# A different order at four places in the start of an attention and FFN kernel on one Trainium2 core

## Chip, core and metric

The kernel runs on one core of a Trainium2 chip. The metric is the device time of one execution, in microseconds (us). Ten runs of the kernel before have a median of 182.95 us (182.34 to 186.69).

## What is computed

Windowed attention with four sink keys, then a feed-forward layer of three matrices of which the elementwise maximum is taken. Cut to what matters:

```python
# batch 4, heads 8, seq 768, head_dim 64; n_sink 4, window 128
scores = (1 / np.sqrt(D)) * np.matmul(q, k.transpose(0, 1, 3, 2))
keep = is_sink | in_window            # key < 4, or 0 <= query - key < 128
scores = np.where(keep, scores, -1e9)
a = np.exp(scores - np.max(scores, axis=-1, keepdims=True))
a = a / (np.sum(a, axis=-1, keepdims=True) + 1e-09)
x = np.matmul(a, v)                   # (B, H, S, D), laid out as 3072 x 512
h = np.maximum(np.maximum(x @ w1, x @ w2), x @ w3)   # 512 x 768 each
out = h @ w_out                       # 3072 x 512
```

Inputs and output are float32; the kernel multiplies in bf16.

## The kernel before

The 3072 tokens are cut into 12 chunks of 256, three to a batch. A chunk goes through these steps, each of which is a letter in strings that write out the order of the work by hand (`step`, L453; `run`, L494). A string such as `"Fb8 Vc Ac0"` with `b=1, c=2` means FFN piece 8 of chunk 1, then the sinks' values of chunk 2, then head pair 0 of chunk 2.

- K, Q (L227, and L240 for the chunks 1 and 2): K and Q are turned on TensorE (PE) into PSUM, and copied to SBUF. K is copied by DVE (VectorE), Q mostly by ACT (ScalarE, L236 and L256).
- B, S (L283, L291): scores of a pair of heads on PE (L306) and their exp on ACT (L312). For the chunks 0 and 1 the mask is added by PE ahead of the scores (L288); later it is multiplied in on DVE (M, L319).
- Z (L321): scores of the sink keys and their exp, for chunks that are not the first of a batch.
- V (L337): eight small matmuls (L345) start four output tiles, one for each head pair, with the sinks' values.
- A (L349): attention times values of a head pair (L358), then on DVE the reciprocal of the sum (L363) and the product that gives x (L366).
- T (L371): x is turned, on PE for the chunks 0 to 4 (L381), by DMA later.
- F (L389): one of nine pieces of the hidden layer, eight matmuls each (L396). The piece's number divided by 3 gives the 256 columns, the rest gives the matrix. The first matrix's result is copied by ACT (L400), the others are joined by a maximum on DVE (L402).
- Y, W (L410): twelve matmuls with w_out (L417) for the two halves of a chunk, copied by ACT (L423) and stored over SP's DMA queue (L407).

The order in the text is the order of issue on every engine: each engine takes its instructions in that order and waits on semaphores for the others. All PSUM tiles come from one pool of eight banks; a tile has to wait until the last reader of its bank's former tile is done.

Transfers go over two queues. SP loads K, Q (L70) and v (L93) of chunk 0, then the rows of v that belong to the sinks (L110). Pool (GpSimd) issues those that cast to bf16 or come early: K and Q of chunks 1 and 2 as `runs` (L84), v of chunks 1 and 2 (L93), the three hidden matrices `w` (L162) and w_out (L170). At the start Pool also makes the identity, the masks (L135 to L146) and, in `sink_v_init` (L178), a selection matrix `sel` (L179, L183) with a column of ones (L180). PE uses `sel` in `sink_v` (L186) to spread the sinks' values over partitions.

`warm(n)` (L124) issues n matmuls of the identity with itself, whose result is not used.

Of the kernel before, what the change touches and what calls it, by code (L numbers as in the profile page):

```python
# [16 lines left out]
def kernel(  # L17
# [33 lines left out]
    with tc.manual_schedule():  # L51
# [26 lines left out]
        def load_runs(ci):  # L78

            b, c = divmod(ci, CPB)  # L80
            t0 = c * 256
            runs[ci] = raw.tile([128, 2, 16 * D], BF16, tag="runs", bufs=2, name="runs")
            for j, src in ((0, k), (1, q)):
                nc.gpsimd.dma_start(  # L84
                    out=runs[ci][:, j],
                    in_=src[b, :, t0:t0 + 256].rearrange("h (r x) d -> h r (x d)", x=16))
            raws[ci] = [None]
# [10 lines left out]
        def load(ci, gate=None):  # L98
            load_qk(ci, gate)
            load_v(ci)  # L100
# [23 lines left out]
        def warm(n):  # L124

            wp = psum.tile([128, 128], F32, tag="f", name="warm")
            for _ in range(n):
                nc.tensor.matmul(wp, lhsT=ident, rhs=ident, start=True, stop=True)  # L128
# [29 lines left out]
        def load_w(wi, lo=0, hi=d_ff):  # L158

            w = (moe_w1, moe_w2, moe_w3)[wi]  # L160
            wt = const.tile([128, DS, hi - lo], BF16, name=f"w{wi}_{lo}")
            nc.gpsimd.dma_start(out=wt, in_=w[:, lo:hi].rearrange("(a p) f -> p a f", p=128))  # L162
            for fb in range(lo // 128, hi // 128):
                w_sb[wi, fb] = wt[:, :, fb * 128 - lo:fb * 128 - lo + 128]
# [3 lines left out]
        def load_wo():  # L168
            for a in range(2):
                nc.gpsimd.dma_start(  # L170
                    out=wo[:, 3 * a:3 * a + 3],
                    in_=moe_w_out[384 * a:384 * a + 384].rearrange("(a p) f -> p a f", p=128))
# [5 lines left out]
        def sink_v_init():  # L178
            nc.gpsimd.memset(sel, 0.0)  # L179
            nc.gpsimd.memset(v_sink[:, :, D:D + 1], 1.0)  # L180
            idv = ident[0:R, 0:R].rearrange("r (s p h) -> r p s h", p=NP, h=2)
            for h in range(2):
                nc.gpsimd.tensor_copy(sel[:, h, :, 0:2 * n_sink].rearrange(  # L183
                    "r p (s h) -> r p s h", h=2)[:, :, :, h], idv[:, :, :, h])

        def sink_v():  # L186
            for h in range(2):
                pv = psum.tile([128, B, D + 1], F32, tag="f", name="vs_ps")
                nc.tensor.matmul(pv, lhsT=sel[:, h].rearrange("r p x -> r (p x)"), rhs=v_sink,
                                 start=True, stop=True)  # L190
                nc.vector.tensor_copy(vs[:, :, h], pv)
# [3 lines left out]
        def cast_qk(ci, j, g, eng):  # L195
            if ci not in bfs:
                bfs[ci] = raw.tile([128, 2, 2, 2, 256], BF16, tag="qk_bf", name="qk_bf")
            src = raws[ci][0][:, j, g].rearrange("p (h i d) -> p h i d", h=4, d=D)
            if ci <= CPB:
                dst = bfs[ci][:, j, g]  # L200
            else:
                dst = bfs[ci][:, j].rearrange("p i a x -> p i (a x)")[:, :, 256 * g:256 * g + 256]
            (eng.tensor_copy if eng else nc.scalar.copy)(  # L203
                dst.rearrange("p i (h d) -> p h i d", d=D), src)
# [10 lines left out]
        def cast(ci):  # L215
            for j, g in ((0, 0), (1, 0), (0, 1), (1, 1)):
                cast_qk(ci, j, g, nc.gpsimd)
            for n in range(2):
                cast_v(ci, n, nc.gpsimd)
# [233 lines left out]
        def step(op):  # L453

            name, ci, arg = op[0], int(op[1:3]), op[3:]
            if ci >= NCH:
                return
            if name in "KQ":
                (prep_runs if ci in runs else prep)(ci, int(name == "Q"), int(arg))
            elif name == "D":  # L460
                turn(ci)
            elif name == "L":
                load(ci)
            elif name == "E":
                place_k(ci, kTs.pop(ci), slice(0, NP))
            elif name == "S":
                score(ci, [int(x) for x in arg])
            elif name == "B":
                score_banks(ci, [int(x) for x in arg])
            elif name == "M":  # L470
                mask(ci, [int(x) for x in arg])
            elif name == "Z":
                if ci % CPB:
                    sink_score(ci)
            elif name == "X":
                if ci % CPB == 0:
                    sink_k(ci // CPB)
            elif name == "V":
                if ci % CPB:
                    sink_av(ci)  # L480
            elif name == "A":
                av(ci, int(arg))
            elif name == "T":
                xpose(ci, int(arg))
            elif name == "F":
                ffn_h(ci, int(arg))
            elif name == "Y":
                ffn_y(ci, [int(arg)], [range(FB)])
            elif name == "W" and ci == NCH - 1:
                ffn_y_end(ci)  # L490
            elif name == "W":
                ffn_y(ci, [0, 1], [range(4), range(4, FB)])

        def run(text, **at):  # L494
            for tok in text.split():
                c = at[tok[1]]
                step(f"{tok[0]}{c:02d}{tok[2:]}")

        sink_v_init()
        load_runs(1)
        load_v(1, nc.gpsimd)
        load_w(0, 0, 256)
        load_w(0, 256, d_ff)
        warm(36)
        cast_qk(0, 0, 0, nc.vector)
        cast_qk(0, 1, 0, nc.vector)
# [18 lines left out]
        load_runs(2)  # L527
        load_v(2, nc.gpsimd)
        load_wo()
        warm(3)  # L530
        run("Aa0 Aa1 Aa2 Aa3 Kb0 Qb0 Ta0 Ta1 Bb01 Sb01 Zb", a=0, b=1)
        sink_v()
        run("Bb23 Sb23 Fa0 Vb Ab0 Ab1 Fa3 Ab2 Ab3 Fa6 Fa1 Tb0 Tb1 Fa4", a=0, b=1)
        cast_v(2, 0, nc.gpsimd)
# [3 lines left out]
            a=0, b=1, c=2)  # L538
# [1 line left out]
        nc.gpsimd.memset(ve[1][:, :, :, D:D + 1], 1.0)  # L540
        cast(3)
        load(4)
        run("Fb5 Sc23 Mc23 Vc Ac0 Fb8 Ac1 Ya0 Ya1", a=0, b=1, c=2)
        cast(4)
        run("Ac2 Ac3 Yb0 Tc0 Tc1 Kd0 Qd0 Yb1 Kd1 Qd1", b=1, c=2, d=3)
        run("Zd Sd0123 Md0123 De Lf", d=3, e=4, f=5)

        for i in range(2, NCH):
# [51 lines left out]
```

## Time and profile before

| What | Value |
|---|---|
| Median of 10 runs | 182.95 us |
| The profiled execution | 183.39 us |
| Its span, first to last instruction | 181.3 us |
| Granted PE clock | 0.995 |
| Chain that ended last, by engine | PE 76%, DMA 11%, SP's queue 3%, ACT 3%, DVE 2% |
| Pool's `sink_v_init` (L179 to L183) | 4.80 to 5.72 us |
| Pool's first five DMA issues | 5.72 to 9.85 us |
| `runs` of Q of chunk 1 land | 13.01 us |
| v of chunk 0 lands | 9.10 us |
| w1, columns 256 to 767, lands | 24.13 us |

The profile is of one execution. A row of a timeline gives the start and the length in us, the engine, the line, the operation, what it writes and reads, how many instructions were merged, and in brackets the idle time of the engine just before and what ended it. PEld is the load of PE's weights, which lies beside its matmuls. The chain of waits is followed back from the last instruction: at each step to what released it, or to the instruction before it on its engine. A row of windows has for each engine the busy time and the number of instructions in that stretch, then the granted PE clock, the mean busy share of the 16 DMA engines (over 1 where packets overlap) and what they moved in GB/s. All times count from the start of the span.

### The profile page before, as it was taken

The page shows a single profiled execution, that of the slowest core. Times are in us where ns is not written, and L with a number is a line of the kernel's source. Part 1 is how long each engine was busy: PE and PEld are TensorE (multiplying, and loading weights), DVE is VectorE, ACT ScalarE, POOL GpSimd, SP SyncE. Part 2 cuts the span into 40 slices and gives each one's busy share as a digit, 9 for nine tenths or more (in the row PEclk, how much of TensorE's full clock was granted, in tenths as well). Part 3 has the DMA queues.
Part 4 walks back from the last instruction along what each step waited for, and adds up shares of the span by engine and source line. Part 5 has one row for each costly group of instructions (what it writes and reads, how often), then busy time and mean ns, then how long its engine had stood idle before and what let it go on. Part 6 is the DMA issues. An engine that isn't in the chain of part 4 may idle for free.

```text
span 181.3 us, 4873 instructions
## 1 busy us (share of the span) xinstructions
PE 170.9 (94%) x1974; PEld 131.9 (73%) x1985; DVE 115.7 (64%) x245; ACT 90.1 (50%) x191; POOL 70.0 (39%) x121
## 2 busy tenths in 40 slices
PE   6969989999999999999999999999999999999991
PEld 6645878775697688588597588687796796796880
DVE  1686435687289289597576676686595786663451
ACT  2447742562971872951933913914736626522220
POOL 7995700657802395454024525326236200000001
PEclk9999999999999999999999999999999999999997
DMA  5999999999599999991789999798999933222404
GB/s 143 237 184 202 208 207 250 199 291 286 151 177 255 189 238 315 250 286 41 141 246 255 148 257 250 154 302 207 130 287 240 125 95 61 45 74 58 116 0 116
DMA packets 64645, 33.63 MB, mean 185 GB/s; under 512 B 26640, under 2 KB 60944, under 8 KB 64624
## 3 DMA queue, kind: packets, MB, share of 16 engines
q1 hardware_dynamic: 59520, 27.70, 65.6%
q0 software_dynamic: 4864, 5.38, 16.5%
q10 hardware_dynamic: 240, 0.26, 0.6%
q8 instruction: 15, 0.25, 0.5%
q14 instruction: 6, 0.05, 0.1%
HBM read 25.20 MB, written 6.29 MB: 174 GB/s over the span
## 4 chain that ended last, share of the span: by engine, by line
PE 76%; DMA 11%; SPq 3%; ACT 3%; issue 2%; DVE 2%; POOL 1%; POOLq 0%; ACTq 0%
PE h_ps L396 49%; PE y_ps L417 15%; DMA w<-in_moe_w_dram 7%; PE o_ps L358 5%; PE st L306 3%; DMA xT<-x_sb 2%; DMA vs_raw<-in_v_dram 2%; ACT e_sb L312 2%; PE y_ps L436 1%; DVE h_sb L402 1%; SPq L110 1%; SPq L70 1%; PE o_ps L345 1%; PE xt_ps L381 1%; PE pt L251 1%
## 5 line engine op out<-in xcount | busy, mean ns | idle before, releaser
L396 PE MATMUL h_ps<-xT,w 128*128 128x256 bf16 x864 | 103.4, 273 | 1.4 <-DMA w<-in_moe_w_dram 0.8
L396 PEld LDWEIGHTS <-w 128*128 128x128 bf16 x864 | 81.1, 98 | 13.6 <-issue 1.6
L402 DVE TENSOR_TENSOR h_sb<-h_sb,h_ps 128x512 bf16<-128x512 bf16 x72 | 49.1, 684 | 27.6 <-PE h_ps L396 23.2
L312 ACT ACTIVATE e_sb<-st 128x512 bf16<-128x512 f32 (+1 forms) x96 | 45.2, 598 | 6.5 <-PE st L306 6.5
L400 ACT CAST h_sb<-h_ps 128x512 bf16<-128x512 f32 x36 | 21.9, 613 | 47.2 <-PE h_ps L396 47.2
L203 POOL CAST qk_bf<-qk_raw 128x512 bf16<-128x512 f32 x36 | 22.4, 630 | 47.0 <-DMA qk_raw<-in_k_dram 27.6
L319 DVE TENSOR_TENSOR e_sb<-e_sb,msk 128x1024 bf16<-128x1024 bf16 (+1 forms) x40 | 28.0, 703 | 18.5 <-ACT e_sb L312 18.2
L212 POOL CAST ve<-v_raw 64x512 bf16<-64x512 f32 x44 | 30.6, 695 | 23.8 <-DMA v_raw<-in_v_dram 19.7
L417 PE MATMUL y_ps<-wo,h_sb 128*128 128x512 bf16 x121 | 30.1, 379 | 0.9
L417 PEld LDWEIGHTS <-h_sb 128*128 128x128 bf16 x132 | 12.4, 97 | 14.1 <-issue 1.1
L366 DVE TENSOR_TENSOR x_sb<-o_ps,rc 128x256 bf16<-128x256 f32 x48 | 20.4, 424 | 1.7
L358 PE MATMUL o_ps<-ve,e_sb 128*128 128x65 bf16 x352 | 17.8, 193 | 1.3 <-DVE ve L212 1.3
L358 PEld LDWEIGHTS <-e_sb 128*128 128x128 bf16 x352 | 15.7, 97 | 3.4 <-issue 0.8
L423 ACT COPY y_sb<-y_ps 128x512 f32<-128x512 f32 x22 | 12.6, 635 | 9.8 <-PE y_ps L417 9.7
L407 POOL DMA_DIRECT2D out_dram<-y_sb x1 | 0.6, 571 | 35.4 <-ACT y_sb L447 35.4
L306 PE MATMUL st<-qT,kk 64*128 64x128 bf16 (+1 forms) x256 | 13.5, 237 | 0.5 <-ACT qT L236 0.3
L306 PEld LDWEIGHTS <-kk 64*128 64x128 bf16 x256 | 8.8, 94 | 4.7 <-issue 2.7
L363 DVE RECIPROCAL rc<-o_ps 128x4 f32<-128x4 f32 x48 | 8.4, 176 | 4.8 <-PE o_ps L358 4.7
L128 PE MATMUL warm<-ident 128*128 128x128 bf16 x43 | 4.7, 298 | 1.4 <-POOL ident masks.py:199 1.4
L330 ACT ACTIVATE e_sink<-sk 128x256 bf16<-128x256 f32 x8 | 3.2, 395 | 5.6 <-PE sk L325 5.6
L256 ACT CAST qT<-pt 128x512 bf16<-128x512 f32 x4 | 2.1, 588 | 7.6 <-PE pt L251 7.6
L383 ACT COPY xT<-xt_ps 128x512 bf16<-128x512 bf16 x8 | 4.3, 594 | 2.1 <-PE xt_ps L381 2.1
(58 smaller groups left out, 76.2 us busy)
## 6 DMA issues: line engine op xcount, KB each, us to landing
out_dram<-y_sb SPq DMA_DIRECT2D x22, 256.0 KB, 4.1
qk_raw<-in_k_dram SPq DMA_DIRECT2D x20, 256.0 KB, 4.0
qk_raw<-in_q_dram SPq DMA_DIRECT2D x20, 256.0 KB, 4.6
v_raw<-in_v_dram SPq DMA_DIRECT2D x10, 512.0 KB, 5.9
v_raw<-in_v_dram POOLq DMA_DIRECT2D x2, 512.0 KB, 10.4
w<-in_moe_w_dram POOLq DMA_DIRECT2D x2, 512.0 KB, 11.4
w<-in_moe_w_dram POOLq DMA_DIRECT2D x1, 768.0 KB, 14.9
wo<-in_moe_w_out_dram POOLq DMA_DIRECT2D x2, 384.0 KB, 14.2
```

The source lines that it names most:

```text
L203: (eng.tensor_copy if eng else nc.scalar.copy)(dst.rearrange("p i (h d) -> p h i d", d=D), src)
L212: (eng.tensor_copy if eng else nc.scalar.copy)(dst[64 * i:64 * i + 64], src[64 * n:64 * n + 64, :, i])
L306: nc.tensor.matmul(st[h][:, sl], lhsT=kx[r, p, k0:k0 + 128], rhs=qx[r], start=ci >= 2, stop=True, skip_group_check=ci < 2)
L312: nc.scalar.activation(e[:, h, lo:], st[:, lo:], AF.Exp, scale=scale)
L319: nc.vector.tensor_tensor(out=e, in0=e, in1=m, op=ALU.mult)
L358: nc.tensor.matmul(o[:, t, h], lhsT=es[ci, p][:, h, sl], rhs=ve[b % 2][:, n, 2 * p + h], start=(c == 0 and x == 0), stop=(x == len(blocks) ...
L366: nc.vector.tensor_mul(xs[ci][:, :, 2 * p:2 * p + 2], o[:, :, :, 0:D], rc.unsqueeze(3).to_broadcast([128, 2, 2, D]))
L396: nc.tensor.matmul(hp[:, f], lhsT=w_sb[wi, 2 * fp + f][:, ds], rhs=xTs[ci][:, :, ds], start=(ds == 0), stop=(ds == DS - 1))
L400: nc.scalar.copy(dst, hp)
L402: nc.vector.tensor_max(dst, dst, hp)
L417: nc.tensor.matmul(yps[ci, t], lhsT=hs[ci][:, fb, t * 128:(t + 1) * 128], rhs=wo[:, fb], start=(fb == 0), stop=(fb == FB - 1))
L423: nc.scalar.copy(y[:, t], yps.pop((ci, t)))
```

## The change

Four things are put in another order, and thirteen warm-up matmuls are added.

```diff
-        sink_v_init()
         load_runs(1)
         load_v(1, nc.gpsimd)
         load_w(0, 0, 256)
         load_w(0, 256, d_ff)
+        sink_v_init()
         warm(36)
...
         load_wo()
-        warm(3)
-        run("Aa0 Aa1 Aa2 Aa3 Kb0 Qb0 Ta0 Ta1 Bb01 Sb01 Zb", a=0, b=1)
+        warm(8)
+        run("Aa0 Aa1 Aa2 Aa3", a=0)
+        warm(8)
+        run("Kb0 Qb0 Ta0 Ta1 Bb01 Sb01 Zb", a=0, b=1)
         sink_v()
...
-        run("Fb5 Sc23 Mc23 Vc Ac0 Fb8 Ac1 Ya0 Ya1", a=0, b=1, c=2)
+        run("Fb5 Sc23 Mc23 Fb8 Vc Ac0 Ac1 Ya0 Ya1", a=0, b=1, c=2)
         cast(4)
-        run("Ac2 Ac3 Yb0 Tc0 Tc1 Kd0 Qd0 Yb1 Kd1 Qd1", b=1, c=2, d=3)
+        run("Ac2 Ac3 Yb0 Tc0 Tc1 Kd0 Qd0 Kd1 Qd1 Yb1", b=1, c=2, d=3)
```

First, Pool makes the selection matrix after it has issued the transfers of chunk 1 and of the first hidden matrix. Second, eight warm-up matmuls instead of three stand ahead of the values of chunk 0 (`Aa`), and eight more between them and the turning of K of chunk 1 (`Kb0`). Third, the last FFN piece of chunk 1 (`Fb8`) stands ahead of the sink values and the first head pair of chunk 2 (`Vc Ac0`). Fourth, the second half of K and Q of chunk 3 (`Kd1 Qd1`) is turned ahead of the second half of y of chunk 1 (`Yb1`).

## Prediction

> **What bounds the kernel now.** I read the page first, then the chain of waits in order of time, then what TensorE (PE) waits for, then the timeline of the three places that the change touches, and last the busy time and DMA traffic in short windows there.
>
> ```profile
> PE 170.9 (94%) x1974; PEld 131.9 (73%) x1985; DVE 115.7 (64%) x245; ACT 90.1 (50%) x191; POOL 70.0 (39%) x121
> ...
> DMA  5999999999599999991789999798999933222404
> ```
>
> PE is busy for 94% of the span, so time comes only out of its few waits. DMA is near full for the first 33 us.
>
> ```profile
> PE o_ps L358 <- DVE ve L212: 1.3, 2, 0.7
> PE h_ps L396 <- DMA w<-in_moe_w_dram: 0.8, 1, 0.8
> PE pt L251 <- DMA runs<-in_q_dram: 0.5, 1, 0.5
> PE st L306 <- ACT qT L236: 0.3, 1, 0.3
> PE o_ps L345 <- DVE h_sb L402: 0.2, 1, 0.2
> ```
>
> Each row: who waited, for what, us in total, times, longest. These are all of PE's waits from 9 to 62 us. Later it waits once more, 0.4 us for a transposed x.
>
> ```profile
> 11.92 12.21 DMA w<-in_moe_w_dram
> 24.13 0.05 issue
> 24.18 7.16 PE h_ps L396 x64
> ```
>
> In the chain the second part of w1 lands at 24.13 and PE goes on at 24.18, after 0.76 us of idling. PE had run out of other work at 23.26, or 23.2 without a wait of 0.1 for w0 at 19.69; so everything before 24.18 has nearly 1 us of slack. From 24.18 the chain is PE nearly without a break. A shift there reaches the end unless a transfer catches it.
>
> **First part: the selection matrix goes behind Pool's first DMA issues.** L179 to L184 take Pool from 4.80 to 5.72, so the five issues (runs of K and Q of chunk 1, v of chunk 1, both parts of w0) move up by 0.92 us. Behind them the last of these issues ends at 8.93 instead of 9.85; the init then runs to 9.85, and the cast of v_sink (9.85 before), the copies of ks and the issues of w1 and w2 follow as before. Were this stretch 0.3 to 0.5 us longer (the four ks copies of 8 columns take 0.98 us beside DVE's casts of v), it would cost nothing: Pool's queue is still moving w0 until 19.65, so the w1 issued at 11.19 waits in line anyhow. The same holds if SP's sink loads, for which that cast waits (landed 9.32), come 0.5 later. `sel` is first read at 15.87.
>
> What do 0.92 us buy? The packets of the trace put the first data of Pool's queue at 7.58 (1.86 us after the issue) and the last of SP's first loads at 8.49. In between the engines fall idle:
>
> ```profile
> 6.50:7.50 1.00, 1.00 (x12) 0.67 (x12) 0.71 (x3) 0.24 (x1) 1.00 (x2) 1.00 1.17 332
> 7.50:8.00 0.50, 0.50 (x12) 0.30 (x9) 0.50 (x2) 0.30 (x1) 0.50 (x1) 1.00 1.29 228
> 8.00:8.50 0.50, 0.50 (x7) 0.33 (x5) 0.34 (x2) 0.50 (x3) 0.50 (x2) 1.00 0.71 138
> 8.50:9.00 0.50, 0.50 (x9) 0.21 (x8) 0.16 (x1) 0.50 (x3) 0.50 (x2) 1.00 0.60 99
> ```
>
> The last two columns are DMA share and GB/s: 332 while SP's queue runs alone, 228 with both, 99 while Pool's first transfer is alone on about half of the engines. Filling the hole at 8 to 9.2 should bring w1 forward by most of the 0.92 us. The bounds are 0.3 (Pool's early packets get in only between SP's) and 0.92; I take 0.7, so w1 would land at 23.4.
>
> Two rules of the Trainium skill speak against it. "SBUF — State Buffer", section "Who interferes with whom", says that a DVE instruction in a two-port mode keeps GpSimd from writing descriptors. The first issue would now start at 4.80, under DVE's cast of 4.69 to 5.12; by the rule 0.32 of the 0.92 us is lost. The rows: the runs' issues took 756 and 712 ns beside DVE casts here, and 642 and 616 ns at 18 us with DVE idle. By the rows the loss is 0.1 per issue, and the early issues pay that already. I follow the rows.
>
> The second matters more. "DMA: Bandwidth & Descriptors", "Queues, rings and completion order", says that each DMA engine goes round-robin between queues that have work. Pool's packets, starting at 6.66, would then take from SP's v of chunk 0, for which DVE waits:
>
> ```profile
> 9.12 1.96 DVE L212 CAST ve<-v_raw 64x512 bf16<-64x512 f32 x4 [0.46 <-DMA v_raw<-in_v_dram]
> 9.21 0.17 PEld L128 LDWEIGHTS <-ident 128*128 128x128 bf16 x3 [0.16 <-issue]
> ```
>
> v lands at 9.10; DVE casts until 11.08, makes x of chunk 0 until 13.71, turns K of chunk 1 until 14.91, and PE scores chunk 1 at 15.10. That chain has no slack, so a late v delays PE by as much. By the rule's equal shares, the 1.05 us of SP data left at 6.66 (702 packets of 512 B, at 85 KB per 0.25 us) takes twice as long: about 1.0 later. By the trace, the 172 packets left at 7.59 (0.3 us of work alone) took 0.9, which is a third of the speed on the slowest engines; if much of that was the small sink loads queued behind, it was two thirds. That gives 0.2 to 1.15 us; no row lies nearer to one end, so I take 0.65. PE would reach the w1 matmuls at 23.2 + 0.65 = 23.85, after w1's landing at 23.4. Part one is thus 23.85 - 24.18 = **-0.33**, and by the bounds from -0.75 (v 0.2 late, w1 decides) to +0.2 (v 1.15 late).
>
> **Second part: more warm-up matmuls.** Warm ones are 57 ns apart (0.17 us for three). Five more before AV of chunk 0 are 0.28 us, in the 0.58 us in which PE waits for `ve` at 9.55 to 10.13. The eight new ones ahead of K of chunk 1 are 0.45 us, at 11.87. Before, K took 11.87 to 12.49 and Q waited for its runs until 13.06. Now K would run 12.32 to 12.94 and Q at once, if its runs land by 12.9 (13.01 less about 0.7). The next step, turning x, waits for DVE until 13.71 anyhow. All this moves with v alike, so I cost it at nothing. Without that cover it would be 0.45. Below nothing it could go only by keeping a clock that would else drop; the granted clock is 1.00 from 5.3 to 175 us, so no such gain is due.
>
> **Third part: the last FFN piece of chunk 1 (Fb8) ahead of AV of chunk 2.**
>
> ```profile
> 38.63 0.23 PE L345 MATMUL o_ps<-vs,e_sink 32*128 32x130 bf16 x2
> 39.10 0.39 PE L345 MATMUL o_ps<-vs,e_sink 32*128 32x130 bf16 x6 [0.24 <-DVE h_sb L402]
> ```
>
> The eight sink matmuls need four PSUM banks. Two are free, the third comes with DVE's max at 39.04, the fourth with an exp at 39.17. From 38.63 to the next matmul at 39.42 pass 0.79 us; the same eight took 0.22 at 18.72. So 0.57 us are lost, of which the wait view shows 0.24. Fb8, now at 39.70, is 0.88 us on PE (8 by 110 ns). Put first, it finds one of the two free banks and runs 38.63 to 39.51. The sink matmuls follow, with the exp's bank long free and the last one coming from Fb5's max at 39.64, 0.1 late. I take **-0.5**, bounds 0 and -0.57. On DVE the max of Fb8 moves ahead of the normalisation of the first two head pairs; that row ends at 43.10 before and after, since the masks hold DVE until 41.40. x of chunk 2 would be ready by about 44.45, when PE comes for it at 44.6.
>
> **Fourth part: K and Q of chunk 3 turned ahead of y of chunk 1.** Eight transposes (0.45 us) swap with six y matmuls (1.3 us).
>
> ```profile
> 47.56 0.59 ACT L423 COPY y_sb<-y_ps 128x512 f32<-128x512 f32 x1
> ...
> 48.05 0.59 ACT L236 COPY qT<-pt 128x512 bf16<-128x512 bf16 x1
> ...
> 48.69 0.51 PE L306 MATMUL st<-qT,kk 64*128 64x256 bf16 x8 [0.28 <-ACT qT L236]
> ```
>
> The second half of the scores waits 0.28 us for the copy of Q, which stood behind ACT's copy of y. Turned early, Q is copied under the y matmuls and the wait goes. But the same ACT time now lies in the copy of y, ahead of the eight exps. The next FFN matmul (49.13) needs the bank that the first exp frees at 49.03. Without the wait PE would come at about 48.8, and the exps start at most 0.05 earlier. So the wait changes its name. I take **-0.05**, bounds 0 and -0.28.
>
> **The sum.** -0.33 + 0 - 0.5 - 0.05 = -0.88 us. The profiled execution took 183.39 (span 181.3, so 2.1 around it); it would be 182.5. The median of the runs is 182.95, and becomes 182.1.
>
> **Rivals.**
> *The start gives nothing* (0.2): v of chunk 0 is late by 0.9 us or more and eats the slack, or a later transfer (xT lands 4.3 us after its issue at 98 us) swallows part. Then some 0.5 is left: 182.45.
> *Fb8 gets the bank of Fb5* (0.1), free at 39.64. It starts at 39.70 as before, with sink and AV work behind it (0.11 + 0.26 + 0.24): y starts at 41.18 instead of 40.81, 0.37 late, which cancels the start: 183.0. Against it: two banks were seen free at 38.63, and the first taker gets one.
> *SP's v is starved* (0.1), the slower end. Where the queues share, Pool's first transfers are served first (16 packets of 173 ns on each of its engines, 2.8 us). v would be some 2.4 us late; 0.9 is slack, 1.5 comes on top, less the 0.55 of the other parts: 183.9. It decides from 1.45 us on. Against it: at 7.6 to 8.5 SP's packets advanced at a third of their speed at worst.
> *As summed* (0.6): 182.1.
>
> About 0.3% (0.55 us) is what a measurement here can tell from no change, so the border is 182.4. Faster: nearly all of the sum's 0.6 and half of the first rival, 0.67; slower: the starved v and a little of the others, 0.12; the rest same. The range reaches from the lower bounds of all parts (-0.75 - 0.57 - 0.28 = -1.6) to a v that is 1.9 late (1.0 beyond the slack, less 0.55: +0.45): 181.4 to 183.4.
>
> **What would show it.** Pool's first issue at 4.80, SP's v landing at 9.3 to 10.3 and the cast at L212 with it; the h_ps matmuls after the turn of x starting near 23.85, with the DMA wait of 0.8 gone or short; eight sink matmuls in about 0.25 us with no DVE wait; no wait on qT at the second half of the scores, but about 0.2 us before the next h_ps. I am wrong if v lands beyond 10.6, if PE shows a new wait of over 0.3 us between 15 and 50 us, or if PE's lead at 50 us is gone by the end.

## The result, and the profile after

The kernel after has a median of 181.19 us (180.65 to 182.56, 15 runs), beside 183.03 (182.21 to 186.69, 50 runs) for the kernel before. The ratio is 0.9907, 95% interval [0.9887, 0.9927]. So it is faster, as forecast, but by 1.7 us (from the ratio) to 1.8 us (from the medians) where 0.88 was forecast, and the time lies below the range of 181.4 to 183.4. The profiled execution took 181.71 us, span 180.0, against 183.39 and 181.3. So the time outside the span fell as well, from 2.1 to 1.7 us. The ratios of this document leave out executions more than 1.5% above the fastest of their kernel; the medians keep them.

The same two rows of the page, and the row of an instruction queue that the prediction did not look at:

```profile
PE 171.7 (95%) x1986; PEld 132.9 (74%) x1998; DVE 116.5 (65%) x245; ACT 90.1 (50%) x191; POOL 69.5 (39%) x121
...
DMA  4999999999599999993789999999999934122404
...
q8 instruction: 15, 0.25, 0.6%
```

PE has a little more to do (the 13 warm-ups) in a span that is 1.3 us shorter. All that PE still waits for between 9 and 70 us, in the view of waits (who, for what, us in total, times, longest):

```profile
PE o_ps L358 <- DVE ve L212: 1.4, 2, 0.8
PE o_ps L345 <- DVE h_sb L402: 0.2, 1, 0.2
```

The waits for w1, for Q's runs and for qT are gone. The sinks' wait for DVE is still there.

**The start.** Pool's timeline:

```profile
4.71 0.76 POOL L84 DMA_DIRECT2D runs<-in_k_dram  x1
5.46 0.61 POOL L84 DMA_DIRECT2D runs<-in_q_dram  x1
6.05 0.95 POOL L93 DMA_DIRECT2D v_raw<-in_v_dram  x1
6.99 1.52 POOL L162 DMA_DIRECT2D w<-in_moe_w_dram  x2
8.55 0.30 POOL L179 MEMSET sel<- 32x256 bf16 x1
...
12.34 0.40 POOL L520 CAST v_sink<-vs_raw 32x256 bf16<-32x256 f32 x1 [3.08 <-DMA vs_raw<-in_v_dram]
```

The issues start where they were expected. The cast of v_sink waits 3.08 us for the sink rows behind SP's v and runs at 12.34 instead of 9.85, so w1 is issued 2.1 us later (13.30, before 11.19). That is more than the 0.3 to 0.5 us for which the prediction had argued that it costs nothing. It costs nothing all the same: w1 lands at 22.51, 1.62 us earlier than before. The chain of waits (start, length) shows what takes the place of w1:

```profile
21.74 1.75 PE h_ps L396 x16
23.48 0.24 PE xt_ps L381 x4
23.72 0.02 issue
23.74 1.08 ACT xT L383 x2
24.82 0.04 issue
24.87 1.14 PE h_ps L396 x9
```

PE reaches the w1 matmuls at 23.77 (forecast 23.85, before 24.18). After the first eight it needs the turned x of chunk 1, which ACT has copied only at 24.82. The next one starts 0.34 us after the eighth, where two usually lie 0.11 apart. That wait was hidden under the wait for w1. By starts of single FFN pieces, the lead is 0.41 us at 23.8 and 0.20 from 26 us on.

**The third and the fourth part.** PE's timeline at the sinks:

```profile
38.44 1.05 PE L396 MATMUL h_ps<-xT,w 128*128 128x256 bf16 x8
39.41 0.23 PE L345 MATMUL o_ps<-vs,e_sink 32*128 32x130 bf16 x3
39.80 0.27 PE L345 MATMUL o_ps<-vs,e_sink 32*128 32x130 bf16 x5 [0.15 <-DVE h_sb L402]
40.00 0.66 PE L358 MATMUL o_ps<-ve,e_sb 128*128 128x65 bf16 x16
```

The eight sink matmuls still take 0.59 us, from 39.41 to 40.00. The y matmuls begin at 40.50, before at 40.81. With the lead of 0.20 taken off, the third part gave 0.11 here on PE's path instead of 0.5. ACT's timeline at the fourth place:

```profile
46.50 1.11 ACT L236 COPY qT<-pt 128x512 bf16<-128x512 bf16 x2
47.70 0.59 ACT L423 COPY y_sb<-y_ps 128x512 f32<-128x512 f32 x1
48.18 1.65 ACT L312 ACTIVATE e_sb<-st 128x384 bf16<-128x384 f32 x4
```

Both copies of Q now stand ahead of the copy of y; the next FFN matmul starts at 48.73 (before 49.13), and the lead is 0.41 us from 53 to 100 us.

**Late in the kernel.** The rest of the gain lies where nothing was changed. The chain at 100 us, of before:

```profile
98.24 4.31 DMA xT<-x_sb
102.55 0.14 issue
102.69 1.36 PE h_ps L396 x11
```

and of after:

```profile
99.56 2.32 PE y_ps L417 x10
101.88 2.19 PE h_ps L396 x20
```

Before, PE stands still for 0.55 us until the x that DMA has turned lands. (I count such a wait as the time from the last y matmul to the next FFN matmul, less the 0.216 that lies between two y matmuls.) Two more such waits, 0.24 us at 154.7 and 0.11 at 166.5, have no row in the view of waits. After, the three are 0.01, 0.00 and 0.02. So of the span's 1.32 us, 0.41 are from the four places and about 0.9 from these waits.

**Outside the span.** The two profiled executions differ by 1.68 us, their spans by 1.32. The rest, some 0.35 us, lies outside the first and last instruction. The experiments say which part it belongs to.

### The profile page after: what moved, and what is told of

Its sections match the earlier page's. It is cut to its first block, busy times and chain, and to the rows that moved or that the text cites. A ratio compares the mean times of both kernels' runs of the same rounds, so it can differ in the third digit from the quotient of the medians.

```text
span 180.0 us, 4899 instructions
## 1 busy us (share of the span) xinstructions
PE 171.7 (95%) x1986; PEld 132.9 (74%) x1998; DVE 116.5 (65%) x245; ACT 90.1 (50%) x191; POOL 69.5 (39%) x121
## 4 chain that ended last, share of the span: by engine, by line
PE 84%; DMA 4%; DVE 4%; ACT 3%; issue 2%; SPq 1%; ACTq 0%
PE h_ps L396 50%; PE y_ps L417 16%; PE o_ps L358 6%; DMA v_raw<-in_v_dram 4%; PE st L306 3%; ACT e_sb L312 2%; DVE h_sb L402 2%; PE y_ps L436 2%; PE pt L251 1%; PE xt_ps L381 1%; SPq L70 1%; PE o_ps L345 1%; PE st L288 1%; DVE ve L212 1%; PE sk L325 1%
## 5 line engine op out<-in xcount | busy, mean ns | idle before, releaser
L319 DVE TENSOR_TENSOR e_sb<-e_sb,msk 128x1024 bf16<-128x1024 bf16 (+1 forms) x40 | 29.5, 744 | 18.7 <-ACT e_sb L312 18.0
L128 PE MATMUL warm<-ident 128*128 128x128 bf16 x56 | 5.9, 287 | 1.4 <-POOL ident masks.py:199 1.4
L128 PEld LDWEIGHTS <-ident 128*128 128x128 bf16 x56 | 5.1, 135 | 1.6 <-POOL ident masks.py:199 1.4
```

What stands on the lines that cost most here:

```text
L319: nc.vector.tensor_tensor(out=e, in0=e, in1=m, op=ALU.mult)
```

## The experiments

Two theories for the part of the gain that I had not forecast. In the expectations they are CLOCK and FETCH.

*Clock.* The ten runs before reach from 182.34 to 186.69. In some executions PE's clock is halved for a while, because PE idles too much ahead of the values of chunk 0. More warm-ups prevent it. (This theory came up after the first four runs.)

*Fetch.* PE reads its instructions through a queue of its own: 15 packets of 16 KB (the row of q8). The times of these packets are in the trace's list of packets, in no view. One lies at 98.3 and one at 152.6 us in before, while x is being turned by DMA. Thirteen more matmuls (26 instructions) bring each fetch forward, to 95.4 and 149.4 in after.

The rivals: the parts give all of it on PE's path, and the late waits are chance (PLACES); or any lead at 24 us brings the later loads forward and so ends the late waits (EARLY).

All runs came in three sets, with 75, 29 and 25 executions of before beside them (medians 183.17, 182.96, 183.20). A halving of 3.4 us takes about 1% off the mean granted clock of an execution (1.7 us of 181), and the half clock at the very end, after PE's last matmul, up to 0.5%; "dropped" counts those below 0.9925.

| Kernel | Median us | Ratio to before [95%] | Dropped | Median of the rest |
|---|---|---|---|---|
| p1_sel: part one alone | 183.01 | 0.9994 [0.9966, 1.0022] | 7 of 22 | 182.70 |
| p2_warm: part two alone | 182.56 | 0.9957 [0.9934, 0.9980] | 0 of 22 | 182.56 |
| p3_fb8: part three alone | 182.40 | 0.9955 [0.9935, 0.9976] | 3 of 22 | 182.21 |
| p4_turn: part four alone | 182.93 | 0.9972 [0.9952, 0.9993] | 4 of 22 | 182.90 |
| before, beside these four | 183.17 | | 19 of 75 | 182.91 |
| a_nosel: after without part one | 181.82 | 0.9935 [0.9915, 0.9956] | 0 of 6 | 181.82 |
| a_nowarm: after without part two | 182.34 | 0.9885 [0.9843, 0.9927] | 4 of 7 | 180.54 |
| c_late13: before, 13 warm-ups at 23 us | 182.71 | 0.9985 [0.9965, 1.0005] | 0 of 22 | 182.72 |
| a_fa7: after, one FFN piece earlier | 181.66 | 0.9924 [0.9894, 0.9953] | 0 of 7 | 181.66 |
| before, beside these four | 182.96 | | 2 of 29 | 182.96 |
| r_after: after, once more | 181.54 | 0.9891 [0.9866, 0.9916] | 0 of 6 | 181.53 |
| p12: parts one and two | 182.31 | 0.9941 [0.9908, 0.9975] | 1 of 10 | 182.04 |
| a_late13: after, part two's 13 at 23 us | 182.14 | 0.9943 [0.9915, 0.9971] | 7 of 16 | 181.30 |
| a_gap16: after, all 16 ahead of AV | 181.71 | 0.9904 [0.9880, 0.9928] | 0 of 6 | 181.72 |
| before, beside these four | 183.20 | | 4 of 25 | 183.05 |

**Each part alone.** p1_sel moves only `sink_v_init`:

```diff
-        sink_v_init()
         load_runs(1)
...
         load_w(0, 256, d_ff)
+        sink_v_init()
```

> The kernel before with the first part alone (selection matrix behind Pool's first issues). Three theories. PLACES: each part gains where it stands, and the 0.9 us by which turned x came late at 102, 155 and 167 us in the profile of before is chance of that one execution. Then the time is 0.2 to 0.3 us under before (ratio 0.9985). FETCH: the late turns of x come from a 16 KB fetch of PE's instructions that falls on them; only the 26 added PE instructions (13 warm-up matmuls with their weight loads) move the fetches. Then this kernel too gains 0.2 to 0.3, and its trace still has a fetch near 98 us and a wait for x of about 0.5 there. EARLY: whatever brings PE forward by 0.3 us at 24 us brings the loads forward and ends the late waits: then 0.9 to 1.2 us faster (ratio 0.994).

The median gains 0.16 us and the ratio's interval covers 1; the executions without a drop gain 0.2, and a third drop. In its trace PE is 1.07 us ahead at 26 us, and at 102 us it waits 0.65 us for the turned x. So a lead alone doesn't end the late waits, which speaks against EARLY.

p2_warm adds only the warm-ups:

```diff
-        warm(3)
-        run("Aa0 Aa1 Aa2 Aa3 Kb0 Qb0 ...
+        warm(8)
+        run("Aa0 Aa1 Aa2 Aa3", a=0)
+        warm(8)
+        run("Kb0 Qb0 ...
```

> The kernel before with the second part alone (13 more warm-up matmuls). PLACES: 0 (between -0.1 and +0.3, since K's turn now has no cover by an early landing of its runs). FETCH: 0.5 to 0.9 us faster (ratio 0.995 to 0.997), with PE's instruction fetch at about 95 us instead of 98 and no wait for turned x at 102. EARLY: 0, with the late waits in place.

This part, which I had costed at nothing, gives 0.6 us in the median, and the interval leaves out 1. Not one of its executions drops, beside 19 of 75 of before. A part of the gain, 0.35 us, remains among executions without a drop. In its trace the late waits are gone.

p3_fb8 and p4_turn:

```diff
-        run("Fb5 Sc23 Mc23 Vc Ac0 Fb8 Ac1 Ya0 Ya1", a=0, b=1, c=2)
+        run("Fb5 Sc23 Mc23 Fb8 Vc Ac0 Ac1 Ya0 Ya1", a=0, b=1, c=2)
...
-        run("Ac2 Ac3 Yb0 Tc0 Tc1 Kd0 Qd0 Yb1 Kd1 Qd1", b=1, c=2, d=3)
+        run("Ac2 Ac3 Yb0 Tc0 Tc1 Kd0 Qd0 Kd1 Qd1 Yb1", b=1, c=2, d=3)
```

> The kernel before with the third part alone (Fb8 ahead of the sink values of chunk 2). PLACES: 0.1 us faster as in the trace of the changed kernel, where the sink matmuls still wait for DVE, up to 0.5 as predicted, where DVE's masks are not slow. FETCH: the same 0.1 to 0.5, late waits for x in place. EARLY: that and about 0.5 more.

> The kernel before with the fourth part alone (K and Q of chunk 3 ahead of y of chunk 1). PLACES and FETCH: 0.05 to 0.1 us faster, not to be told from no change; the score's wait for Q is gone and the next FFN matmul waits for the first exp instead. EARLY: the same, since 0.1 us brings little forward.

Part three gives 0.8 us in the median and 0.7 without drops. Part four gives 0.2 in the median and 0.01 without drops, though its ratio's interval just leaves out 1. The median changes of the four alone add up to 1.8 us; those without drops to 1.3 (0.21, 0.35, 0.70, 0.01), their means to 1.7 (0.34, 0.40, 0.70, 0.24).

The 0.7 of part three is more than its bound of 0.57, and half of it is not on PE's path. In the 85 executions of kernels with part three, the time less the span is 1.66 to 1.77 us. In the 227 of those without it (the three sets of before, p1_sel, p2_warm, p4_turn, c_late13, p12), it is 2.01 to 2.14. The lists of packets show one place where the two groups differ: a last packet of the kind "instruction", 8 KB, begins about 1.6 us after the end of the span in the six traces without part three, and 1.12 to 1.16 us after it in those with it (0.31 in a_fa7). Why the order of Fb8 does that stays open.

**The change without part one, and without part two.** a_nosel and a_nowarm take one part back:

```diff
+        sink_v_init()
         load_runs(1)
...
-        sink_v_init()
```

> The changed kernel without its first part (selection matrix made ahead of Pool's issues, as before). CLOCK and PLACES: the wait for w1 of 0.5 to 0.7 us near 24 us is back, 0.2 to 0.6 slower than the changed kernel (181.5 to 181.8). EARLY: a larger loss, about 1 us. If the first part is worth nothing even with the warm-ups beside it, as it was alone (ratio 0.9994), 181.2.

```diff
-        warm(8)
-        run("Aa0 Aa1 Aa2 Aa3", a=0)
-        warm(8)
-        run("Kb0 Qb0 Ta0 Ta1 Bb01 Sb01 Zb", a=0, b=1)
+        warm(3)
+        run("Aa0 Aa1 Aa2 Aa3 Kb0 Qb0 Ta0 Ta1 Bb01 Sb01 Zb", a=0, b=1)
```

> The changed kernel without its second part (warm-up matmuls as before). New theory CLOCK: with v of chunk 0 landing 1 us later PE idles longer around 9.5 to 12 us, and in a part of the executions the clock is then granted at half for 3.4 us (as in the trace of the kernel with the third part alone, 12.3 to 15.7); the added warm-ups stop that. Then this kernel is 0.5 to 1.2 us slower than the changed one (182.0 or more), with a wide spread of times (over 2.5 us), and where its trace catches it the clock falls back to half. FETCH: 0.3 to 0.5 slower, with a fetch of PE's instructions at about 152 us and late x there, no wide spread. PLACES: as the changed kernel, 181.2 (ratio 0.990).

Beside the other parts, part one looks worth more than alone: the ratio is 0.9935 without it and 0.9907 and 0.9891 with it. But these are of different sets and their intervals overlap, so it isn't shown. The wait for w1 is back in the trace of a_nosel, with 0.4 us. Without part two the executions fall in two groups: 180.21, 180.54 and 180.82 us at clocks of 0.996 to 1.0, and 182.34 to 183.88 at 0.985 to 0.99. The three without a drop are no slower than the kernel after (181.19), so they show no worth of part two beyond the drops. The ratio in the table leaves out the two longest, so the two groups tell more. Its profiled execution (182.8) is of the second group. Its windows, laid from the moment at which the clock rose, in steps of the length of the drop:

```profile
6.88:10.29 3.41, 3.26 (x38) 1.88 (x37) 3.14 (x8) 2.72 (x8) 2.53 (x7) 1.00 1.00 190
10.29:13.71 3.42, 1.73 (x67) 1.49 (x68) 2.91 (x11) 0.93 (x3) 1.23 (x6) 1.00 1.13 245
13.71:17.12 3.41, 3.41 (x46) 1.96 (x40) 1.73 (x4) 1.07 (x2) 3.26 (x6) 0.50 1.30 206
```

The same for after:

```profile
7.23:10.64 3.41, 3.09 (x39) 1.90 (x37) 1.85 (x7) 2.55 (x8) 1.98 (x6) 1.00 1.12 184
10.64:14.06 3.42, 2.33 (x88) 2.13 (x90) 2.91 (x10) 0.76 (x2) 1.68 (x7) 1.00 1.15 246
14.06:17.47 3.41, 3.36 (x53) 1.79 (x48) 2.84 (x8) 2.23 (x5) 3.26 (x5) 1.00 1.30 201
```

Where PE was busy for 1.73 of 3.42 us (51%), the clock is 0.50 in the next window; with 2.33 (68%) it holds. The trace of p3_fb8 has a drop too, from 12.26 to 15.68 us after a window with 1.79 of 3.41 (52%). These are the two lowest shares among the windows up to 20 us of all 14 traces; p1_sel and p12 had 54 and 55% and kept the clock, before 61%. The moment at which the clock first rises differs from one execution to the next (4.1 to 7.2 us), so the windows fall differently over the same gap, and a kernel near the border drops in a part of its executions. This is the Trainium skill's free-running window of 3413 ns ("TensorE: Matmul & The Clock Gate", Part 1). The page has the clock halve after an idle window, warns of gaps of more than about 3.4 us, and tells of a kernel in which frequent short idling did it. Here the longest times between two matmul starts in those windows were 0.84 and 1.12 us (p12 kept the clock with 1.53), and a half-busy window was enough.

The busy share alone is not the border, though. In the last windows of the kernel, after keeps the clock with 47%, while before loses it with 41%:

```profile
174.48:177.90 3.42, 1.61 (x15) 1.19 (x13) 1.27 (x3) 0.37 (x1) 0.57 (x1) 1.00 0.39 100
177.90:181.31 3.41, 0.00 (x0) 0.00 (x0) 0.00 (x0) 0.00 (x0) 0.00 (x0) 1.00 0.17 56
```

```profile
175.99:179.40 3.41, 1.38 (x13) 0.98 (x11) 1.17 (x3) 0.37 (x1) 0.57 (x1) 1.00 0.46 122
179.40:181.33 1.93, 0.00 (x0) 0.00 (x0) 0.00 (x0) 0.00 (x0) 0.00 (x0) 0.50 0.17 56
```

a_nosel keeps it with 47 and a_gap16 with 43%. There each matmul has 128x128 weights and 256 columns; in a_nowarm's half-busy window it has 65 columns, or weights of 128x64. An estimate that counts this sorts all windows with matmuls, from the first rise of the clock on, of the 14 traces. It takes for each matmul record the share of 128x128 that its weights fill, times its columns at 0.42 ns each (a y matmul's 0.216 us by 512). By it the seven windows that were followed by half the clock have 9 to 35% of the array in use (a_nowarm's 35, p3_fb8's 30), and all others 37% or more. It was found in these same traces, and no run tested it.

**Fetches without the early warm-ups.** c_late13 leaves the start of before alone and puts 13 warm-ups into the wait for w1, where they cost little:

```diff
-        run("Bb23 Sb23 Fa0 Vb Ab0 Ab1 Fa3 Ab2 Ab3 Fa6 Fa1 Tb0 Tb1 Fa4", a=0, b=1)
+        run("Bb23 Sb23 Fa0 Vb Ab0 Ab1 Fa3 Ab2 Ab3 Fa6 Fa1 Tb0 Tb1", a=0, b=1)
+        warm(13)
+        run("Fa4", a=0)
```

> The kernel before with 13 more warm-up matmuls (26 PE instructions), put where PE waits for w1 near 23.5 us. They shift PE's instruction fetches as the second part does, but keep no clock at 9 to 15 us. FETCH: 0.3 to 0.6 us faster than before (ratio 0.997), the fetch at 95 and 150 us, x not late at 102 and 155. CLOCK: 0 to 0.2 slower (the wait for w1 doesn't cover them in every execution); the clock drops remain. PLACES: 0.

The fetches move (94.1 and 149.6 us) and the late waits are gone in its trace. The time falls by 0.25 us, but the interval reaches 1, so a gain isn't shown. None of its 22 executions dropped, but only 2 of 29 of before did in that set, so it says nothing on the clock. a_late13 makes the same edit in after, in place of part two:

> The changed kernel with its 13 extra warm-up matmuls taken from the start and put ahead of the FFN piece Fa4 (about 23 us): TensorE fetches as many instructions as after, but the idle stretch ahead of AV of chunk 0 has only three warm-ups again. Clock and fetch theory: the clock drops in a third to a half of the executions (those 182.3 to 184), the others 181.0 to 181.7 (the 13 cost up to 0.5 where they stand now), and the wait of 0.26 for the turned x at 155 us that the kernel without part two showed is gone. If only the fetches matter: no drops, all at 181.2 to 181.7. If the clock alone matters and the fetches nothing: drops as said, and the wait of about 0.26 at 155 us is there.

It tests the two theories apart. Seven of 16 executions drop (182.53 to 184.32), since the start has three warm-ups again; the others have a median of 181.30, and the wait at 155 us is gone, with the extra instructions in place. The chain of a_nowarm at that place:

```profile
150.80 0.99 PE st L306 x24
151.79 0.02 issue
151.81 2.75 PE y_ps L417 x12
154.56 0.10 issue
154.66 2.34 PE h_ps L396 x20
```

From the first of twelve y matmuls to the next FFN matmul pass 2.85 us. In a_late13:

```profile
150.41 0.02 issue
150.43 0.38 PE y_ps L417
150.80 0.05 issue
150.85 2.32 PE y_ps L417 x10
153.18 2.62 PE h_ps L396 x24
```

Here it is 2.59 by the starts of the single matmuls (150.43 to 153.01; the chain's pieces begin where the one before ends), which is 12 by 0.216: no wait. So it is in all traces at this place: the five kernels without extra PE instructions (before, p1_sel, p3_fb8, p4_turn, a_nowarm) wait 0.24 to 0.45 us and fetch at 151.1 to 152.6; the nine with them wait 0.00 and fetch at 147.7 to 150.6. x is turned by two transposes. In the five, the fetch starts after the first has landed (2.42 to 2.44 us after its issue), and the second takes 4.08 to 4.29. In the nine, the fetch starts while the first is under way, which then takes 3.46 to 4.06, and the second 3.06 to 3.61; both are done 4.3 to 4.9 us after the first issue, instead of 5.3 to 5.6. That 26 more instructions take this wait away, wherever they stand, is shown; that the fetch packet itself holds a transpose up fits these times and was not tried by itself.

At 102 us it is otherwise. p3_fb8, p4_turn and a_nowarm, without extra instructions, don't wait there (0.00), although a fetch starts at 97.1 to 97.6 with the first transpose under way or just ahead of it; a_nosel, r_after and p12, with them, wait 0.13, 0.26 and 0.69. So the count of instructions doesn't decide the largest of the three waits. What does stays open.

**The change once more, and with less.**

> The changed kernel once more, beside the three below. If its gain of 1.7 us is what the earlier runs say (a clock that no longer drops, about 0.4 on the median; instruction fetches moved off the transposes of x, about 0.3; the rest the four parts on TensorE's path), it comes to 181.1 to 181.6 with no execution below 0.9925 of granted clock, and its trace shows no wait of over 0.1 for the turned x at 102 and 155 us. If the gain was luck of the first executions: 182 or more, with such waits back.

r_after repeats the gain: 0.9891 [0.9866, 0.9916], and no execution drops. One expectation failed: its trace waits 0.26 us at 102 us, where its x lands at 101.42. Its lead over before is larger there (0.85 us) than that of the first trace, and the landing of x swallows a part.

p12 leaves parts three and four out, with their two lines as they were before:

```diff
-        run("Fb5 Sc23 Mc23 Fb8 Vc Ac0 Ac1 Ya0 Ya1", a=0, b=1, c=2)
+        run("Fb5 Sc23 Mc23 Vc Ac0 Fb8 Ac1 Ya0 Ya1", a=0, b=1, c=2)
...
-        run("Ac2 Ac3 Yb0 Tc0 Tc1 Kd0 Qd0 Kd1 Qd1 Yb1", b=1, c=2, d=3)
+        run("Ac2 Ac3 Yb0 Tc0 Tc1 Kd0 Qd0 Yb1 Kd1 Qd1", b=1, c=2, d=3)
```

> Parts one and two of the change without three and four. Theory: part one makes v of chunk 0 a microsecond later, TensorE idles longer, and without more warm-up matmuls the clock halves for 3.4 us in a third of the executions; part two prevents that, so together they give more than the sum of their single ratios (0.9994 and 0.9957): 0.9925 to 0.994, 181.6 to 181.9, no execution with a dropped clock. Rival, the parts simply add: 0.995 to 0.996, 182.1 to 182.3. Rival, part two is worth only its moved fetches: 0.997 to 0.998.

0.9941 with an interval from 0.9908 to 0.9975 covers both the sum of the two parts and more than it: undecided. One execution in ten had a clock of 0.991, so even with the warm-ups the border can be crossed.

**Two tries for a faster version.** a_gap16 puts all 16 warm-ups ahead of AV of chunk 0, since the chain of after has the second eight on it (0.45 us at 12.80). a_fa7 issues another FFN piece of chunk 0 to cover the new wait at 24.5 us:

```diff
-        warm(8)
-        run("Aa0 Aa1 Aa2 Aa3", a=0)
-        warm(8)
-        run("Kb0 Qb0 Ta0 Ta1 Bb01 Sb01 Zb", a=0, b=1)
+        warm(16)
+        run("Aa0 Aa1 Aa2 Aa3 Kb0 Qb0 Ta0 Ta1 Bb01 Sb01 Zb", a=0, b=1)
```

> The changed kernel with all 16 warm-up matmuls ahead of AV of chunk 0, none ahead of K of chunk 1. If what holds the clock is a shorter idle stretch before AV, no execution drops and the time is that of the changed kernel or 0.1 to 0.3 less (181.0 to 181.4), since K and Q of chunk 1 come 0.45 sooner where nothing needs them sooner. If the second eight hold it (the drop seen without them began at 13.7 us), a fifth to a half of the executions drop and the median is 181.5 to 182.3.

```diff
-        run("... Tb0 Tb1 Fa4", a=0, b=1)
+        run("... Tb0 Tb1 Fa4 Fa7", a=0, b=1)
...
-        run("Fb0 Fb3 Fb6 Fb1 Fb4 Fa7 Fb7 ...
+        run("Fb0 Fb3 Fb6 Fb1 Fb4 Fb7 ...
```

> The changed kernel with Fa7 (FFN piece 7 of chunk 0, the same w1 columns) moved up to follow Fa4, so that it covers the copy of turned x of chunk 1, for which PE waits 0.2 us at 24.7 in the changed kernel. All theories: 0.1 to 0.2 us faster than the changed kernel (181.0) unless the lead is lost later to the DMA of x at about 101.6, where all kernels so far landed it; then no difference from 181.2.

Neither can be told from the kernel after (181.19 and 181.54). a_fa7 has the shortest span of all traces, 178.7, but its median doesn't show it.

## Why the forecast was right in sign and too small

Two steps of the prediction failed: part two was costed at nothing, and the time around the span was taken as fixed.

**Part two at nothing: wrong.** Alone it gives 0.6 us (0.9957 [0.9934, 0.9980]). The step that failed is "the granted clock is 1.00 from 5.3 to 175 us, so no such gain is due". That is one execution. Of before, 25 of 129 dropped, and a dropped one takes 0.6 to 1.2 us more (184.10 against 182.91 in the first set, 183.64 against 183.05 in the third). Dropped executions lift the median of before by 0 to 0.26 us. With part one in and no part two it is 18 of 45 (p1_sel, a_nowarm, a_late13), at a price of 2.2 us in a_late13 (183.52 against 181.30). With part two it is 1 of 72, seven kernels taken together. So that part two prevents drops is shown. What else its 26 instructions bring is not settled: p2_warm without drops says 0.35 us, c_late13 0.25 with an interval that reaches 1, and the three executions of a_nowarm without a drop were no slower than the kernel after. That the kernel's times before reached up to 186.69 was there to be read.

**2.1 us around the span: not fixed.** The prediction added its sum to the time of the profiled execution, "span 181.3, so 2.1 around it". In every kernel with part three it is 1.7, so 0.35 us of the gain lie where the prediction didn't look. The -0.88, with 0.4 for part two without drops (the mean) and this 0.35, comes to -1.6.

**Part one, -0.33: the sign right, both terms mis-sized.** "v lands late by 0.65" was 1.03 in the trace of after, near the bound. But it isn't a constant: the cast of v starts at 8.85, 8.95, 8.98, 9.01, 9.01, 9.44, 10.16 and 10.43 us in the eight traces with part one, and at 8.87 to 9.66 in the six without it. In most executions SP's v loses nothing to Pool's queue. The prediction's own sum was wrong here too. By equal shares the 1.05 us of data from 6.66 would end at 8.76, which is 0.27 later than the 8.49 of before, not 1.0. A third and two thirds of the speed give 1.3 late and not late, instead of 1.15 and 0.2. A delay of 0.27 can't be told from the scatter, so these rows decide nothing about the rule of equal shares. "w1 lands 0.7 earlier, at most 0.92" was 1.62 in this pair. Before's 24.13 is the latest of all: w1 lands at 22.0 to 23.5 us with part one and at 22.8 to 24.1 without, on average 0.95 earlier. That PE reached w1 at 23.77, beside 23.85 in the forecast, is luck: v came later than forecast, but by 23.3 us PE had only 0.51 of the 1.03 left (23.26 to 23.77). What then ends the wait is ACT's copy of the turned x, which the prediction didn't name.

**Part three, -0.5: right on PE's path where DVE's mask runs alone.** In a_late13 the step comes out as written:

```profile
39.20 0.30 PE L345 MATMUL o_ps<-vs,e_sink 32*128 32x130 bf16 x8
39.43 0.66 PE L358 MATMUL o_ps<-ve,e_sb 128*128 128x65 bf16 x16
```

Eight sink matmuls in 0.23 us, no wait; a_nosel, a_nowarm and a_fa7 have the same. In after, r_after, p3_fb8 and a_gap16 they take 0.59 to 0.67 us, because the max of Fb5, which frees the last bank, is late by one slow mask. Pool's timeline in after:

```profile
36.59 0.82 POOL L203 CAST qk_bf<-qk_raw 128x512 bf16<-128x512 f32 x1 [0.20 <-DMA qk_raw<-in_q_dram]
```

and DVE's:

```profile
35.89 2.06 DVE L319 TENSOR_TENSOR e_sb<-e_sb,msk 128x1024 bf16<-128x1024 bf16 x2 [0.82 <-ACT e_sb L312]
37.88 1.87 DVE L402 TENSOR_TENSOR h_sb<-h_sb,h_ps 128x512 bf16<-128x512 bf16 x3
```

The two masks end at 37.95; by its own row the second starts at 36.87, with 0.54 us of Pool's cast (36.59 to 37.41) still to come, and takes 1.08 us. In a_late13 only 0.19 us of the cast were left, and that mask took 0.73. "SBUF — State Buffer", "Who interferes with whom", says that a DVE instruction with both inputs in SBUF contends with a GpSimd instruction that reads it; these rows agree. When Pool casts depends on when chunk 3's K and Q land, so whether this gain is 0.1 us or less, or 0.5, is decided anew in each execution.

**Part four, -0.05: right.** The wait for qT is gone, the next FFN matmul comes about 0.1 us sooner, and alone the executions without a drop differ by 0.01 us by medians and 0.24 by means.

**The late waits: missed.** The prediction saw the first ("0.4 us for a transposed x") and asked only whether such a place could swallow a lead. In the trace of before it cost 0.55 us, and in that of after nothing. It swallows leads as well: in p1_sel PE came 0.65 us ahead of x, which landed at 101.8. In p12 x landed at 102.8, and PE waited 0.69. The count of PE's instructions decides the wait at 155 us, by the traces; it doesn't decide this one.

What stays open is the exact split of the 1.7 us. Without drops the four parts alone add up to 1.3 by medians and 1.7 by means, and the kernel after is 1.5 ahead of such executions of before in the third set (181.53 against 183.05), or 1.8 by means. So the parts may simply add; that they help each other is not shown.

## What to carry to other kernels

One profile is one draw: read the spread of the times and the granted clock of every execution before an edit that only keeps PE busy is costed at nothing. An edit that fills PE's idle time ahead of the steady part can pay in the executions in which the clock would drop. When a lead is carried to the end, look for the next place that waits on a transfer, and ask what else shifts with the number of instructions. Compare the spans as well as the times: a change of order moved the time outside the span here.

## What the runs showed of the hardware

- Early in the kernel, a window of 3.41 us with PE busy for 51 or 52% was followed by half the clock for exactly the next window; 54% and more was not. At its end 43 and 47% kept the clock, with matmuls that use more of the array. By the estimate above, the border lies between 35 and 37% of the array in use.
- PE fetches its instructions in 15 packets of 16 KB in 180 us. At 155 us, where a fetch starts between the landings of two DMA transposes, the second lands 4.08 to 4.29 us after its issue; where it starts ahead of both landings, 3.06 to 3.61. The skill's "Runtime: NRT & Kernel Launch", "Instruction fetch mechanics", calls the cost of a block mostly hidden. That holds for PE itself here: from 6 us on no row of its waits (0.15 us or more) names anything but DVE, ACT or a transfer of data.
- The time outside the first and last instruction was 1.66 to 1.77 us in 85 executions with one order of PE's work, and 2.01 to 2.14 in 227 with another.
- A mask multiplication of 0.69 us on DVE took 1.08 to 1.13 us when 0.54 to 0.59 us of a Pool cast were left at its start, and 0.73 with 0.19 left (after, r_after, p3_fb8; a_late13).
- The landing of the first transfer of v, issued at 2.96 us in every trace, varies from 8.8 to 10.4 us between the 14 traces.
